# Seven block products in place of eight in units 1 to 7 of layer 2 of an FFT and two-layer MLP kernel

## Chip, cores and metric

One NeuronCore of a Trainium2 chip runs the kernel. The metric is the device time of one execution in microseconds (us); the number compared is the median over runs. Before the change it was 1027.38 us, the median of three runs from 1026.6 to 1029.3.

## What is computed

```python
X = np.fft.fft(np.fft.fft(x, axis=1), axis=2).real        # x: 2 x 3008 x 256
x = X.reshape(6016, 256)
h = x @ w_in                                              # layer 1, 256 x 2048
g = np.where(h >= 1, h, np.where(h <= -1, 0.0, (h + 1) ** 2 / 4))
x = g @ w_out                                             # 2048 x 256
h = x @ w_in2                                             # layer 2, 256 x 2048
g = np.maximum(0.01 * h, h)
return g @ w_out2                                         # 2048 x 256
```

## The kernel before

**Tiling.** Everything is held with features on the partitions and tokens along the free dimension. The 6016 tokens are 8 units of 752 (UT), each two halves of 376 columns (H4). The 2048 hidden features are 16 tiles of 128 (NF), called f. A step n is one f tile of one unit: layer 1 has steps 0 to 127 (N1 = 128), layer 2 steps 128 to 255. The Fourier transform comes first, in an order written out by hand, and its second stage is folded into layer 1's weights.

**Precision.** An fp32 operand is split into a rounded part ("high", type fp32r) and the difference ("low"). A product of two operands is three matmuls: high by high, high by low, low by high. So one 128 x 128 block of weights against one 128 x 376 block of tokens costs three matmuls.

**One step of layer 2** (`layer_2`, L672 on). `first_2` puts 12 matmuls (L556: two halves, two blocks of the 256 inputs, three each) into a pair of PSUM banks q. ScalarE writes 0.01 q to the SBUF tile s (L678), VectorE takes the maximum of q and s (L679). `high` (L574) rounds the step before on ScalarE, `low` (L578) forms its difference on GpSimd. `second` adds step n - 4 (LAG = 4) with 12 matmuls (L569) into four PSUM banks acc, which hold 256 outputs x 752 tokens of a unit; after the last f tile of a unit `store` copies them out, two on ScalarE (L597) and two on VectorE (L598). In layer 1 the copies stay in SBUF (tile y) and `split_y` (L606 on ScalarE, L607 on VectorE) makes the operands of layer 2; in layer 2 they go to the output by DMA.

**Layer 1's step** (`layer_1`) has 6 matmuls for its first product (L545), 12 for the second (L569), three VectorE operations on PSUM (L653, L656, L657), three activations on ScalarE and VectorE's maximum (L666).

**Order.** The kernel is under a manual schedule: every engine executes its instructions in the order in which they are written, and waits by semaphore where a tile isn't ready or a buffer isn't free. Side work hangs on a table `jobs`: `plan_at` puts a piece of work behind a given step. In layer 1 the second layer's first weights are loaded, converted from the 64-bit words in which they come (L210 to L223) and spilled to DRAM; from step 122 on `rf` reads them back, and L257 (ScalarE) and L261 (VectorE) split them into wc. The last weights (wd) are converted from step 125 to step 143 (L271 ScalarE, L275 VectorE).

**Buffers that the change touches.** Pool ps_ab has two pairs of PSUM banks, ps_acc four single banks; that is all eight. t3 holds three generations of gh and gl, t5 four tiles s, `by` eight units of the first layer's operands and later y, rw four tiles for loads.

Of the kernel before, what the change touches and what calls it, by code (L numbers as in the profile page):

```python
# [19 lines left out]
P = 128  # L20
# [138 lines left out]
def fnet_moe_kernel(ctx: ExitStack, tc: tile.TileContext, xpq, dft_e, dft_o, dft_d, pick,  # L159
# [23 lines left out]
    wb = {}  # L183
    bt = {}
# [49 lines left out]
    def first_weights(j):  # L234


        c = ToF32()
        t = {}

        def spill():  # L240
            c.rest()
            t["dram"] = sp.tile([P, 512], F32, name=f"w3f{j}")
            nc.sync.dma_start(out=t["dram"], in_=c.f32)

        def load():
            t["f32"] = rw.tile([P, 512], I64, tag="rw", name="rf").bitcast(F32)[:, :512]
            nc.sync.dma_start(out=t["f32"], in_=t["dram"])

        def views():
            v = t["w"].rearrange("p q (h e) f -> p q h e f", e=2)  # L250
            s = t["f32"].rearrange("p (q h f) -> p q h f", q=2, h=2)
            return [(v[:, q, :, 0, :], v[:, q, :, 1, :], s[:, q]) for q in range(2)]

        def high():
            t["w"] = new_wa(j, "wc")
            for hi, _, s in views():
                A.copy(hi, s)  # L257

        def low():
            for hi, lo, s in views():  # L260
                V.tensor_tensor(out=lo, in0=s, in1=hi.bitcast(F32), op=ALU.subtract)  # L261
            wa[j] = t["w"]

        return [lambda: c.load(w3, j), c.begin, c.exponent, c.sign, spill, load, high, low]
# [16 lines left out]
    with tc.manual_schedule():  # L281
# [249 lines left out]
        A.activation(warm[:, :1], warm[:, :1], CLAMP, scale=15.5)  # L531
# [5 lines left out]
        gh, gl, acc, yh, hp, rp, gp = {}, {}, {}, {}, {}, {}, {}  # L537
# [38 lines left out]
        def low(n):  # L576
            gl[n] = t3.tile([P, 2, H4], FR, tag="gl", name="gl")
            G.tensor_tensor(out=gl[n], in0=gp.pop(n), in1=gh[n].bitcast(F32), op=ALU.subtract)  # L578

        def store(n, first):  # L580

            u = n % N1 // NF
            if first:
                yt[u] = by.tile([P, 2, 2, H4], F32, tag="by", name=f"y{u}")
                dst = [yt[u][:, m] for m in range(2)]
            else:
                dst = [to.tile([P, 2, H4], F32, tag="o", name=f"o{u}{m}") for m in range(2)]
            if u == NU - 1 and not first:
                half = H4 // 2
                A.copy(dst[0][:, 0], acc[0][:, :H4])  # L590
                V.tensor_copy(dst[0][:, 1], acc[1][:, :H4])
                A.copy(dst[1][:, 0], acc[2][:, :H4])
                V.tensor_copy(dst[1][:, 1, :half], acc[3][:, :half])
                A.copy(dst[1][:, 1, half:], acc[3][:, half:H4])
# [178 lines left out]
```

## Time and profile before

| what | value |
| --- | --- |
| median of three runs | 1027.38 us (1026.6, 1027.38, 1029.3) |
| span of the profiled execution | 1029.2 us |
| TensorE (PE) busy | 1009.1 us, 98% of the span |
| weight loads (PEld) busy | 975.8 us, 95% |
| VectorE (DVE) | 610.2 us, 59% |
| ScalarE (ACT) | 623.7 us, 61% |
| GpSimd (POOL) | 491.8 us, 48% |

The profiled execution's own time isn't listed apart from its span; the highest of the three times, 1029.3, is 0.1 above that span. The shares are means over stages: the Fourier part fills about the first 110 us, layer 1 runs to about 500 us, layer 2 from there to the end. Matmuls overlap in the trace, so the mean duration of a matmul (334 ns) is longer than the time from one to the next; a stretch's time divided by its count gives that pace.

### The profile page before, as it was taken

Reading aid. Unit: us, or ns where it says so; the run is one execution under the profiler, and the core shown is the slowest. Engines: PE = TensorE matmul, PEld = TensorE weight load, DVE = VectorE, ACT = ScalarE, POOL = GpSimd, SP = SyncE. Lnnn points to the kernel's source line nnn. Section 1 sums busy time; section 2 is a strip of 40 time slices with the busy share of each in tenths; the row PEclk is TensorE's granted clock in tenths of the full one; section 3 lists DMA queues with packets and bytes.
Section 4 is the critical chain, followed back from the end, with each engine's and each line's share of the span. In section 5 each row is a group of like instructions: output and inputs, shape, how many; then the busy total and the mean of one; then the engine's idle time right before and its main releaser. Section 6 shows DMA issues by size and latency. Waiting matters only on the chain.

```text
span 1029.2 us, 14547 instructions
## 1 busy us (share of the span) xinstructions
PE 1009.1 (98%) x5660; PEld 975.8 (95%) x5660; DVE 610.2 (59%) x916; ACT 623.7 (61%) x975; POOL 491.8 (48%) x270
## 2 busy tenths in 40 slices
PE   7998999999999999999999999999999999999998
PEld 5657899999999999999999999999999999999998
DVE  5689999888888888888897232232323223232221
ACT  4357889888888888887775444444444444344443
POOL 1002876565655565655554444444444444444443
PEclk9799999999999999999999999999999999999999
DMA  9841000000100010101220000000000000000000
GB/s 298 295 129 62 1 1 21 12 32 2 42 11 11 32 32 2 52 1 62 82 93 1 32 1 31 1 1 31 1 7 24 1 31 2 1 31 1 31 1 31
DMA packets 12165, 39.25 MB, mean 38 GB/s; under 512 B 1472, under 2 KB 1472, under 8 KB 11840
## 3 DMA queue, kind: packets, MB, share of 16 engines
q1 hardware_dynamic: 11088, 34.79, 9.5%
q0 software_dynamic: 864, 3.15, 1.7%
q8 instruction: 44, 0.72, 0.3%
q10 hardware_dynamic: 144, 0.39, 0.1%
q14 instruction: 25, 0.20, 0.1%
HBM read 30.06 MB, written 8.26 MB: 37 GB/s over the span
## 4 chain that ended last, share of the span: by engine, by line
PE 88%; DVE 6%; ACT 3%; DMA 1%; issue 1%; ACTq 0%; DVEq 0%; SPq 0%
PE acc L569 47%; PE q L556 25%; PE p L545 11%; PE do L461 2%; DMA rw<-in_w_dram 1%; DVE r L666 1%; DVE tw L218 1%; DVE aa L653 1%; PE dc L426 1%; PE ds L427 1%; DVE h L656 1%; PE g L339 1%; DVE cw L223 1%; ACT gh L574 1%; DVE h L657 1%
## 5 line engine op out<-in xcount | busy, mean ns | idle before, releaser
L578 POOL TENSOR_TENSOR gl<-s,gh 128x752 fp32r<-128x752 f32 x128 | 235.0, 1836 | 288.8 <-ACT gh L574 288.8
L578 POOL TENSOR_TENSOR gl<-r,gh 128x752 fp32r<-128x752 f32 x128 | 243.7, 1904 | 188.6 <-ACT gh L574 129.0
L679 DVE TENSOR_TENSOR s<-q,s 128x752 f32<-128x752 f32 x128 | 120.2, 939 | 302.4 <-ACT s L678 302.2
L556 PE MATMUL q<-yh,wc 128*128 128x376 f32 x1536 | 284.7, 334 | 0.0
L569 PE MATMUL acc<-gh,wb 128*128 128x376 f32 x1024 | 281.1, 335 | 0.2
L569 PE MATMUL acc<-gh,wd 128*128 128x376 f32 x1024 | 278.9, 334 | 0.5 <-DVE y L598 0.5
L556 PEld LDWEIGHTS q<-yh,wc 128*128 128x128 f32 x1536 | 265.7, 188 | 0.0
L574 ACT CAST gh<-s 128x752 fp32r<-128x752 f32 x128 | 105.2, 822 | 146.3 <-PE acc L569 146.3
L569 PEld LDWEIGHTS acc<-gh,wb 128*128 128x128 f32 x1024 | 186.7, 188 | 3.3 <-ACT r L663 2.2
L569 PEld LDWEIGHTS acc<-gh,wd 128*128 128x128 f32 x1024 | 186.6, 188 | 0.8 <-DVE y L598 0.8
L678 ACT ACTIVATE s<-q 128x752 f32<-128x752 f32 x128 | 102.4, 800 | 138.6 <-PE q L556 138.6
L569 PE MATMUL acc<-gl,wb 128*128 128x376 f32 x512 | 172.1, 336 | 4.6 <-POOL gl L578 4.6
L569 PE MATMUL acc<-gl,wd 128*128 128x376 f32 x512 | 171.2, 334 | 0.0
L545 PE MATMUL p<-bt,wa 127*128 127x376 f32 (+3 forms) x768 | 154.5, 336 | 2.2 <-DVE bsc L484 1.4
L545 PEld LDWEIGHTS p<-bt,wa 128*128 128x128 f32 (+1 forms) x768 | 134.6, 189 | 3.7 <-ACT tw L210 1.7
L666 DVE TENSOR_TENSOR r<-h,r 128x752 f32<-128x752 f32 x128 | 127.7, 998 | 0.2 <-ACT r L670 0.2
L670 ACT ACTIVATE r<-r 128x752 f32<-128x752 f32 x128 | 106.8, 834 | 4.1
L569 PEld LDWEIGHTS acc<-gl,wb 128*128 128x128 f32 x512 | 96.3, 188 | 7.4 <-POOL gl L578 7.3
L574 ACT CAST gh<-r 128x752 fp32r<-128x752 f32 x128 | 103.2, 807 | 0.1
L659 ACT ACTIVATE r<-h 128x376 f32<-128x376 f32 x128 | 66.2, 517 | 60.2 <-DVE h L656 55.7
L653 DVE SCALAR_TENSOR_TENSOR aa<-ct,g,p 128x376 f32<-128x376 f32 (+1 forms) x128 | 77.3, 604 | 42.0 <-PE p L545 41.8
L569 PEld LDWEIGHTS acc<-gl,wd 128*128 128x128 f32 x512 | 96.0, 187 | 0.0
(79 smaller groups left out, 654.6 us busy)
## 6 DMA issues: line engine op xcount, KB each, us to landing
rw<-in_w_dram SPq DMA_DIRECT2D x32, 512.0 KB, 3.9
out_dram<-o SPq DMA_DIRECT2D x15, 376.0 KB, 2.8
x<-in_xpq_dram SPq DMA_DIRECT2D x6, 512.0 KB, 6.3
x<-in_xpq_dram POOLq DMA_DIRECT2D x6, 512.0 KB, 7.6
me<-in_dft_e_dram SPq DMA_DIRECT2D x4, 567.0 KB, 15.4
mo<-in_dft_o_dram SPq DMA_DIRECT2D x2, 1128.0 KB, 19.6
w3f<-cw SPq DMA_DIRECT2D x8, 256.0 KB, 2.2
rf<-w3f SPq DMA_DIRECT2D x8, 256.0 KB, 2.7
```

What stands on the lines that cost most here:

```text
L461: T.matmul(pe[:m, par, :H4], lhsT=weights(blk, lo, hi), rhs=mat[lo:hi, blk, c, :], start=(c == par and blk == 0), stop=(c == 2 and blk == 1))
L545: T.matmul(p[:, j, :n], lhsT=w[:m, 2 * j + x, :], rhs=b[:m, 2 * j + y, :n], start=(a == 0), stop=(a == 2))
L556: T.matmul(p[:, t, :H4], lhsT=w[:, 2 * d + x, :], rhs=y[d][:, z, t, :], start=(a == 0), stop=(a == 5))
L569: T.matmul(acc[k][:, :H4], lhsT=w[:, x, m * P:(m + 1) * P], rhs=y[:, t, :], start=(f == 0 and i == 0), stop=(f == NF - 1 and i == 2))
L574: A.copy(gh[n], gp[n])
L578: G.tensor_tensor(out=gl[n], in0=gp.pop(n), in1=gh[n].bitcast(F32), op=ALU.subtract)
L653: V.scalar_tensor_tensor(out=aa[:, :w], in0=ct[u][:, :w], scalar=g128[:, f:f + 1], in1=p[:, 0, :w], op0=ALU.mult, op1=ALU.add)
L659: A.activation(r[:, 0], h[:, 0], CLAMP, scale=15.5)
L666: V.tensor_tensor(out=g, in0=hp.pop(n - 1), in1=g, op=ALU.max)
L670: A.activation(r, r, AF.Square, scale=0.5 / 15.5, bias=0.5)
L678: A.activation(g, p, AF.Copy, scale=0.01)
L679: V.tensor_tensor(out=g, in0=p, in1=g, op=ALU.max)
```

## The change

Layer 2's first product treats two f tiles together. Its operands then are 2 x 2 blocks: the weights a11, a12, a21, a22 (f tile by input block) and the tokens b11, b12, b21, b22 (input block by half). Instead of eight block products it forms seven, with sums of weights s1 to s4 and sums of tokens t1 to t4:

- s1 = a21 + a22, s2 = s1 - a11, s3 = a11 - a21, s4 = a12 - s2
- t1 = b12 - b11, t2 = b22 - t1, t3 = b22 - b12, t4 = b21 - t2
- bank x collects a11 b11, then s2 t2, then s3 t3, then a22 t4; bank v collects s1 t1, then s4 b22; bank y holds a12 b21
- ScalarE copies x after its first product and v after its first product (tile av), and x after its second (tile bb); VectorE adds: h1 = (y + av, v + bb), second half of h2 = x + av; the last x is the first half of h2

This holds for units 1 to 7 (`layer_2_pair`, one call for two steps). Unit 0 keeps eight products (`layer_2`); its `low` runs on VectorE instead of GpSimd. The leaky maximum becomes one activation on ScalarE (`leaky`), VectorE's L679 is gone. Layer 1's result goes to DRAM and comes back as rows (`store`, `load_y`); GpSimd forms t1 to t4 (`mix_y`), ScalarE and VectorE split the seven operands of a unit (`split_high`, `split_low`). The weights' plain parts are kept by a DMA (`keep`), the rows are loaded a second time, VectorE forms s1 to s4 (`sum_1`, `sum_2`), and they are split (`mixed_high`, `mixed_low`). The accumulators are allocated once. `store` gives banks 0 and 1 to VectorE and banks 2 and 3 to ScalarE. From step 144 on the two PSUM pairs are four single banks, three of them used by a call of `layer_2_pair`. The clamp of layer 1 uses another saturating identity (limit 240 in place of 15.5, scales changed to match).

```diff
-            for hi, _, s in views():
-                A.copy(hi, s)
+        def high_of(key, nm):
+            t[key] = wp.tile([P, 4, 2, P], FR, tag="wa", name=f"{nm}{j}")
+            A.copy(t[key][:, :, 0, :], blocks(t["f32"])[:, t["at"]:t["at"] + 4])
+        def low_of(key):
...
+        def keep():
+            wt[j] = tri[j // 4].tile([P, 3, 2, P], FR, tag="wt", name=f"wt{j}")
+            nc.sync.dma_start(out=wt[j].bitcast(F32), in_=t["plain"][:, 0:3].bitcast(F32))
+        def sum_1():
+            V.tensor_tensor(out=s1, in0=a21, in1=a22, op=ALU.add)
+            V.tensor_tensor(out=s3, in0=a11, in1=a21, op=ALU.subtract)
+        def sum_2():
+            V.tensor_tensor(out=s2, in0=s1, in1=a11, op=ALU.subtract)
+            V.tensor_tensor(out=s4, in0=a12, in1=s2, op=ALU.subtract)
...
-        A.activation(warm[:, :1], warm[:, :1], CLAMP, scale=15.5)
+        A.activation(warm[:, :1], warm[:, :1], HOLD, scale=240.0)
...
+        def product(bank, w, y, start):
+            for a, (x, z) in enumerate(((0, 0), (0, 1), (1, 0))):
+                T.matmul(bank[:, :H4], lhsT=w[:, x, :], rhs=y[:, z, :], start=start and a == 0, stop=a == 2,
+                         skip_group_check=not start)
-        def second(n, f):
-            if f == 0:
+        def second(n, f, ks=range(4)):
+            if not acc:
...
-        def low(n):
+        def low(n, engine=G):
...
                 for t in range(2):
-                    A.copy(dst[0][:, t], acc[t][:, :H4])
-                    V.tensor_copy(dst[1][:, t], acc[2 + t][:, :H4])
+                    if part == 0:
+                        V.tensor_copy(o[:, t], acc[t][:, :H4])
+                    else:
+                        A.copy(o[:, t], acc[2 + t][:, :H4])
...
+        def mix_y(u, i):
+            b11, b12, b21, b22 = yr[u][:4]
...
+            out, x, y = ((t1, b12, b11), (t2, b22, t1), (t3_, b22, b12), (t4, b21, t2))[i]
+            G.tensor_tensor(out=out, in0=x, in1=y, op=ALU.subtract)
+        def split_high(u, i):
...
+            A.copy(ops[u][i // 2][:, i % 2, 0], yr[u][(0, 4, 5, 3, 6, 2, 7)[i]])
+        def split_low(u, i):
+            y = ops[u][i // 2][:, i % 2]
+            V.tensor_tensor(out=y[:, 1], in0=yr[u][(0, 4, 5, 3, 6, 2, 7)[i]], in1=y[:, 0].bitcast(F32),
+                            op=ALU.subtract)
...
-            plan_at(N1 - 6 + 2 * j, *zip((0, 3, 3), w3s[j][5:]))
-            plan_at(N1 - 3 + 2 * j, *zip((0, 1, 2, 2, 3, 4, 4), w4s[j]))
+            plan_all(N1 - 6 + 2 * j, (0, 3, 3, 4), plain)
+            plan_all(N1 + 8 + 2 * j, (0, 2, 3, 4, 5), mixed)
+            plan_at(N1 - 3 + 2 * j, *((x, k, s) for x, k, s in zip((0, 1, 2, 2, 3, 4, 4), "SSAVVAV", w4s[j])))
...
         for u in range(1, NU):
-            for d in range(2):
-                plan_at(N1 + NF * (u - 1) + 8 + 3 * d, (0, lambda u=u, d=d: split_y(u, d)))
+            plan_at(N1 + NF * (u - 1), (3, "S", lambda u=u: load_y(u)),
+                    *((5 + i, "G", lambda u=u, i=i: mix_y(u, i)) for i in range(4)),
+                    *((7 + i, "A", lambda u=u, i=i: split_high(u, i)) for i in range(7)),
+                    *((7 + i, "V", lambda u=u, i=i: split_low(u, i)) for i in range(7)))
...
-                A.activation(g, p, AF.Copy, scale=0.01)
-                V.tensor_tensor(out=g, in0=p, in1=g, op=ALU.max)
+        def leaky(out, h):
+            A.activation(out, h, AF.Prelu, alpha=0.01)
+        def layer_2(n):
...
+            leaky(g, p[:, :, :H4])
+            if n > N1:
+                high(n - 1)
+                low(n - 1, V)
+            sums(n)
+        def layer_2_pair(n):
+            new = n < 2 * N1
+            m1, m2 = n - 3, n - 2
...
+                product(x, a11, b11, True)
+                product(v, s1, t1, True)
+                A.copy(av[:, 0], x[:, :H4])
+                A.copy(av[:, 1], v[:, :H4])
+            todo(n, "S")
+            todo(n + 1, "S")
+            sums_of(m1, 0)
+            if last_x:
+                h, xp = last_x.pop()
+                leaky(h[:, 0], xp[:, :H4])
+                leaky(h[:, 1], h[:, 1])
+            if new:
+                product(x, s2, t2, False)
+                A.copy(bb, x[:, :H4])
+                product(v, s4, b22, False)
+                V.tensor_tensor(out=h1[:, 1], in0=v[:, :H4], in1=bb, op=ALU.add)
+            if n - 1 in gp:
+                high(n - 1)
+                low(n - 1)
+            sums_of(m1, 1)
+            todo(n, "AG")
+            if new:
+                product(x, s3, t3_, False)
+                V.tensor_tensor(out=h2[:, 1], in0=x[:, :H4], in1=av[:, 1], op=ALU.add)
+                product(y, a12, b21, True)
+                V.tensor_tensor(out=h1[:, 0], in0=y[:, :H4], in1=av[:, 0], op=ALU.add)
+            todo(n, "V")
+            sums_of(m2, 0)
+            if new:
+                leaky(h1, h1)
+                high(n)
+                low(n)
+            sums_of(m2, 1)
+            todo(n + 1, "AG")
+            if new:
+                product(x, a22, t4, False)
+                last_x.append((h2, x))
+            todo(n + 1, "V")
```

**Where the instructions stand now.** TensorE in a step of layer 2, before (wc the weights, yh the tokens of `first_2`; the same four rows and twelve of `second` make every step):

```order
L556 MATMUL q_4_8026<-yh_7660,wc_5191 128x376 x3
L556 MATMUL q_4_8026<-yh_7759,wc_5191 128x376 x3
L556 MATMUL q_4_8026<-yh_7660,wc_5191 128x376 x3
L556 MATMUL q_4_8026<-yh_7759,wc_5191 128x376 x3
L569 MATMUL acc_0_8046<-gh,wd_5184 128x376
L569 MATMUL acc_0_8046<-gl,wd_5184 128x376
L569 MATMUL acc_0_8046<-gh,wd_5184 128x376
```

and the start of a call of `layer_2_pair` (wt plain weights, ws summed ones, op the seven token operands):

```order
L581 MATMUL x_9276<-op_8531,wt_5602 128x376 x3
L581 MATMUL v_9278<-op_8531,ws_6208 128x376 x3
L592 MATMUL acc_798<-gh,wd_5549 128x376
L592 MATMUL acc_798<-gl,wd_5549 128x376
L592 MATMUL acc_798<-gh,wd_5549 128x376
L592 MATMUL acc_799<-gh,wd_5549 128x376
L592 MATMUL acc_799<-gl,wd_5549 128x376
L592 MATMUL acc_799<-gh,wd_5549 128x376
L581 MATMUL x_9276<-op_8606,ws_6208 128x376 x3
L581 MATMUL v_9278<-op_8606,ws_6208 128x376 x3
```

The seven products of three now stand in four places between the pieces of `second`, 21 and 24 matmuls in one call where two steps had 24 and 24; the whole program has 5377 matmuls instead of 5545.

ScalarE in three steps of layer 2, before:

```order
L678 ACTIVATE s<-q_4_8026 128x752
L574 CAST gh<-s 128x752
L678 ACTIVATE s<-q_5_8062 128x752
L574 CAST gh<-s 128x752
L678 ACTIVATE s<-q_6_8094 128x752
L574 CAST gh<-s 128x752
```

and in one call of `layer_2_pair` (two steps), without side work:

```order
L807 COPY av<-x_7059 128x376
L808 COPY av<-v_7061 128x376
L753 ACTIVATE s<-x_6990 128x376
L753 ACTIVATE s<-s 128x376
L818 COPY bb<-x_7059 128x376
L597 CAST gh<-s 128x752
L753 ACTIVATE s<-s 128x752
L597 CAST gh<-s 128x752
```

Two steps had four instructions of 752 columns here; one call has three of 752 and five of 376. Three of the copies read a bank that TensorE goes on adding to.

VectorE in the first unit of layer 2, two steps before:

```order
L679 TENSOR_TENSOR s<-q_8_5456,s 128x752
L218 SCALAR_TENSOR_TENSOR tw<-rw,tw 128x512
L223 SCALAR_TENSOR_TENSOR cw<-rw,tw 128x512
L607 TENSOR_TENSOR yh_5493<-y_1905,yh_5493 128x752
L679 TENSOR_TENSOR s<-q_9_5496,s 128x752
L275 TENSOR_TENSOR wd_5528<-cw,wd_5528 128x2x256
L214 TENSOR_SCALAR tw<-tw 128x512
L261 TENSOR_TENSOR wc_5535<-rf,wc_5535 128x2x128 x2
```

and two steps now:

```order
L601 TENSOR_TENSOR gl<-s,gh 128x752
L277 TENSOR_TENSOR rf<-rf 128x128
L278 TENSOR_TENSOR rf<-rf 128x128
L220 SCALAR_TENSOR_TENSOR tw<-rw,tw 128x512
L225 SCALAR_TENSOR_TENSOR cw<-rw,tw 128x512
L665 TENSOR_TENSOR op_5561<-ry,op_5561 128x376
L601 TENSOR_TENSOR gl<-s,gh 128x752
L282 TENSOR_TENSOR rf<-rf 128x128
L283 TENSOR_TENSOR rf<-rf 128x128
L305 TENSOR_TENSOR wd_5639<-cw,wd_5639 128x2x256
L216 TENSOR_SCALAR tw<-tw 128x512
L260 TENSOR_TENSOR wc_5646<-rf,wc_5646 128x4x128
```

The maximum is replaced by the difference gl; the sums of weights and the splits of the tokens of unit 1 have come in between. ScalarE's order has one ACT_TABLE_LOAD, at its start, before and now.

## Rows read from the trace of the kernel before

**Rows 1.** Page, parts 1 and 2: busy time, and TensorE's granted clock in 40 slices.

```profile
PE 1009.1 (98%) x5660; PEld 975.8 (95%) x5660; DVE 610.2 (59%) x916; ACT 623.7 (61%) x975; POOL 491.8 (48%) x270
PEclk9799999999999999999999999999999999999999
```

**Rows 2.** Busy time by stage: stretch, its length, engines (instructions), clock, DMA share, GB/s.

```profile
0.00:110.00 110.00, 97.39 (x391) 69.80 (x392) 85.13 (x180) 58.46 (x116) 18.06 (x16) 0.94 0.57 183
300.00:400.00 100.00, 99.93 (x578) 99.06 (x577) 85.64 (x142) 84.19 (x139) 60.27 (x32) 1.00 0.06 20
506.60:1024.90 518.30, 518.12 (x3012) 517.81 (x3012) 182.08 (x191) 230.67 (x307) 229.53 (x126) 1.00 0.05 18
600.00:700.00 100.00, 100.00 (x584) 100.00 (x583) 29.30 (x29) 42.55 (x54) 43.72 (x25) 1.00 0.02 9
```

**Rows 3.** Page, part 4: the chain that ended last, by engine.

```profile
PE 88%; DVE 6%; ACT 3%; DMA 1%; issue 1%; ACTq 0%; DVEq 0%; SPq 0%
```

**Rows 4.** TensorE groups by line: busy, mean ns, idle before and what ended it.

```profile
L556 PE MATMUL q<-yh,wc 128*128 128x376 f32 x1536 | 284.7, 334 | 0.0
```

**Rows 5.** Timeline inside layer 2: start, length (us), instruction, idle before.

```profile
645.07 2.23 PE L556 MATMUL q<-yh,wc 128*128 128x376 f32 x12
645.26 0.82 ACT L574 CAST gh<-s 128x752 fp32r<-128x752 f32 x1 [1.20 <-PE acc L569]
646.23 1.82 POOL L578 TENSOR_TENSOR gl<-s,gh 128x752 fp32r<-128x752 f32 x1 [2.31 <-ACT gh L574]
647.39 0.80 ACT L678 ACTIVATE s<-q 128x752 f32<-128x752 f32 x1 [1.30 <-PE q L556]
```

**Rows 6.** ScalarE groups by line, shapes apart.

```profile
L597 ACT COPY o<-acc 128x376 f32<-128x376 f32 x14 | 5.9, 473 | 0.0
L659 ACT ACTIVATE r<-h 128x376 f32<-128x376 f32 x128 | 66.2, 517 | 60.2 <-DVE h L656 55.7 <-POOL gl L578 3.0 <-issue 0.2
L670 ACT ACTIVATE r<-r 128x752 f32<-128x752 f32 x128 | 106.8, 834 | 4.1
L574 ACT CAST gh<-s 128x752 fp32r<-128x752 f32 x128 | 105.2, 822 | 146.3 <-PE acc L569 146.3
```

**Rows 7.** VectorE and GpSimd groups by line, shapes apart.

```profile
L656 DVE TENSOR_TENSOR h<-aa,p 128x376 f32<-128x376 f32 x128 | 69.9, 546 | 4.4
L505 DVE TENSOR_TENSOR bt<-bs,bt 128x376 fp32r<-128x376 f32 x4 | 2.0, 548 | 0.2
L666 DVE TENSOR_TENSOR r<-h,r 128x752 f32<-128x752 f32 x128 | 127.7, 998 | 0.2 <-ACT r L670 0.2
L382 DVE TENSOR_TENSOR xt<-pc 126x129 f32<-126x129 f32 x12 | 3.4, 286 | 0.0
L578 POOL TENSOR_TENSOR gl<-s,gh 128x752 fp32r<-128x752 f32 x128 | 235.0, 1836 | 288.8 <-ACT gh L574 288.8
```

**Rows 8.** Timeline of GpSimd and VectorE at the start of layer 2.

```profile
505.20 1.86 POOL L578 TENSOR_TENSOR gl<-s,gh 128x752 fp32r<-128x752 f32 x1 [1.10 <-ACT gh L574]
505.29 0.93 DVE L679 TENSOR_TENSOR s<-q,s 128x752 f32<-128x752 f32 x1
507.05 0.68 DVE L275 TENSOR_TENSOR wd<-cw,wd 128x512 fp32r<-128x512 f32 x1
507.65 0.42 DVE L214 TENSOR_SCALAR tw<-tw 128x512 int32<-128x512 int32 x1
514.18 1.84 POOL L578 TENSOR_TENSOR gl<-s,gh 128x752 fp32r<-128x752 f32 x1 [2.07 <-ACT gh L574]
514.59 1.97 DVE L275 TENSOR_TENSOR wd<-cw,wd 128x512 fp32r<-128x512 f32 x1 [1.08 <-ACT wd L271]
```

**Rows 9.** Timeline of TensorE and VectorE where layer 2's first sums begin.

```profile
506.14 0.99 DVE L598 COPY y<-acc 128x376 f32<-128x376 f32 x2
506.73 0.44 PE L569 MATMUL acc<-gh,wd 128*128 128x376 f32 x1 [0.48 <-DVE y L598]
```

**Rows 10.** Page, part 6: loads of weight words, KB each, median us to landing.

```profile
rw<-in_w_dram SPq DMA_DIRECT2D x32, 512.0 KB, 3.9
```

More of the change, by code (lines that the diff above doesn't have):

```diff
@@ L183, in fnet_moe_kernel @@
     wb = {}
+    wt = {}
+    tri = []
     bt = {}
@@ L245, in load @@
         def load():
[L246 to L252, printed above, removed]
+            t["f32"] = rw.tile([P, 512], I64, tag="rw", name="rf").bitcast(F32)
+            nc.sync.dma_start(out=t["f32"][:, :512], in_=t["dram"])
@@ L259, in low @@
         def low():
[L260 to L264, printed above, removed]
+            low_of("plain")
+        def keep():
+            wt[j] = tri[j // 4].tile([P, 3, 2, P], FR, tag="wt", name=f"wt{j}")
+            nc.sync.dma_start(out=wt[j].bitcast(F32), in_=t["plain"][:, 0:3].bitcast(F32))
+        def sum_1():
+            a11, a12, a22, a21, s1, s2, s3, s4 = (blocks(t["f32"])[:, i] for i in range(8))
+            V.tensor_tensor(out=s1, in0=a21, in1=a22, op=ALU.add)
+            V.tensor_tensor(out=s3, in0=a11, in1=a21, op=ALU.subtract)
@@ new lines, in sum_2, with mixed_high, mixed_low @@
+        def sum_2():
+            a11, a12, a22, a21, s1, s2, s3, s4 = (blocks(t["f32"])[:, i] for i in range(8))
+            V.tensor_tensor(out=s2, in0=s1, in1=a11, op=ALU.subtract)
+            V.tensor_tensor(out=s4, in0=a12, in1=s2, op=ALU.subtract)
+        def mixed_high():
+            t["at"] = 4
+            high_of("mixed", "ws")
+        def mixed_low():
+            low_of("mixed")
+        return ([("S", lambda: c.load(w3, j)), ("A", c.begin), ("V", c.exponent), ("V", c.sign), ("V", spill)],
+                [("S", load), ("A", high), ("V", low), ("S", keep)],
+                [("S", load), ("V", sum_1), ("V", sum_2), ("A", mixed_high), ("V", mixed_low)])
@@ L574, in high, with store @@
             A.copy(gh[n], gp[n])
-        def low(n):
+        def low(n, engine=G):
             gl[n] = t3.tile([P, 2, H4], FR, tag="gl", name="gl")
-            G.tensor_tensor(out=gl[n], in0=gp.pop(n), in1=gh[n].bitcast(F32), op=ALU.subtract)
-        def store(n, first):
+            engine.tensor_tensor(out=gl[n], in0=gp.pop(n), in1=gh[n].bitcast(F32), op=ALU.subtract)
+        def store(n, part):
             u = n % N1 // NF
[L583 to L588, printed above, removed]
-                half = H4 // 2
[L590 to L594, printed above, removed]
+            first = n < N1
+            last = u == NU - 1 and not first
+            if part == 0:
+                ot[u] = [to.tile([P, 2, H4], F32, tag="o", name=f"o{n // NF}{m}") for m in range(2)]
+            o = ot[u][part]
+            if last and part == 0:
+                A.copy(o[:, 0], acc[0][:, :H4])
+                V.tensor_copy(o[:, 1], acc[1][:, :H4])
+            elif last:
+                half = H4 // 2
+                A.copy(o[:, 0], acc[2][:, :H4])
+                V.tensor_copy(o[:, 1, :half], acc[3][:, :half])
+                A.copy(o[:, 1, half:], acc[3][:, half:H4])
@@ new lines, in store, with load_y @@
+            if first:
+                yt[u, part] = sp.tile([P, UT], F32, name=f"y{u}{part}")
+            queue = nc.scalar if last and part else nc.sync
+            queue.dma_start(out=yt[u, part] if first else out[part, :, u * UT:(u + 1) * UT],
+                            in_=o.rearrange("p t n -> p (t n)"))
+        def load_y(u):
+            yr[u] = []
+            for d in range(2):
+                if u == 1:
+                    y = th.tile([P, 2, H4], F32, tag="h", name="ry").rearrange("p t n -> p (t n)")
+                else:
+                    y = rw.tile([P, 512], I64, tag="rw", name="ry").bitcast(F32)[:, :UT]
+                nc.sync.dma_start(out=y, in_=yt[u, d])
+                yr[u] += [y] if u == 0 else [y[:, :H4], y[:, H4:]]
```

168 lines of the change are left out of this document (102 added, 66 removed).

## Prediction

> **What bounds the kernel now.** I read the page first. TensorE is busy for 98% of the span, the other engines for 48 to 61% [rows 1]; the reader is to see that one engine is full and that its clock stands at the top digit (2.4 GHz) in all slices but the second. Busy time alone does not say what paces it, so the table by stage comes next [rows 2]: in the first 110 us TensorE has 97.39 busy us and the clock is 0.94; in layer 1, 99.93 of 100 with VectorE and ScalarE at some 85; in layer 2, 100.00 of 100, VectorE at 29 and ScalarE at 43. Layer 2 is where the change lies, and there nothing but TensorE can be the bound. The chain that ended last says the same, PE 88% [rows 3], and the first product's group has no idle time in front of it over 1536 matmuls [rows 4].
>
> So the price of a matmul is read from this stretch: 3012 of them from 506.60 to 1024.90 us in 518.12 us, **172.0 ns each**. (The groups' mean of 334 ns is no price: matmuls overlap.) Weight loads are busy as long as matmuls; each matmul has its own, so both counts fall together. A step of 24 is 4.13 us, two steps 8.26.
>
> **What is removed.** Per call of the new function, three matmuls of 48. There are 7 units x 8 calls = 56 calls, so 168 matmuls, as the programs' counts of 5545 and 5377 say too. 168 x 172.0 ns = **28.9 us**. A call has 45 matmuls, 7.74 us. All else is worth what it makes TensorE wait.
>
> **ScalarE in a call.** Copies av, av and bb from PSUM, 376 columns: 3 x 0.473 (the eviction at L597). The leaky function on two halves: nothing in the trace ran it. Its nearest rows are other functions of the same size: 0.473 for a copy from PSUM, 0.517 for the clamp, 0.834 for the square on 752 [rows 6]. I take these, since clamp, square and copy hardly differ; below them I see no reason for a gain, above them the trace gives no end, and that end is a rival. So 0.47 + 0.52 + 0.83, and two casts of 0.822. Sum 4.88 us. No table load comes with it, since the order has one, as before. Side work per call: seven split casts of a unit, priced as the clamp, 7 x 0.517 / 8 = 0.45, and two output copies, 2 x 0.473 / 8 = 0.12. In all 5.45 of 7.74 us: covered.
>
> **The new waits, by position in a call.** From one engine's end to the next one's start the trace shows 0.09 us (TensorE to ScalarE, 647.30 to 647.39) and 0.15 us (ScalarE to GpSimd, 646.08 to 646.23) [rows 5]; I take 0.15. Position k is k x 0.172 us after the call's start.
> - Bank x is done at position 3 (0.52), copied from 0.67 to 1.14; TensorE adds s2 t2 to it at position 12 (2.06). Bank v: done 1.03, copied to 1.65, needed at position 15 (2.58). The second copy of x: done at 2.58, copied 2.73 to 3.20, needed at position 24 (4.13). Margins 0.92, 0.93, 0.93 us. What could fill ScalarE at that time: the cast of the call before ends at 7.81, a split cast at 8.33, which is 0.59 into this call; and the two leaky halves from 1.65 to 2.65. They fit, just.
> - The add from x after s3 t3 (position 27, 4.64) ends by 5.34 with 0.546 for a VectorE operation on PSUM [rows 7]; TensorE needs the bank at 42 (7.22).
> - The chain behind h1: bank y at position 30 (5.16), add to 5.86, leaky to 6.84, cast to 7.81, GpSimd's difference of 1.836 to 9.8; its first reader stands 30 matmuls into the next call, at 12.9. Margin 3.1. Behind h2: casts end at about 4.0 of the next call, the difference at 6.0, read at 8.9. Margin 2.9.
>
> VectorE has 3 x 0.546 + 7 x 0.548 / 8 and two evictions per unit, some 2.3 us a call; GpSimd 2 x 1.836 and four small differences per unit, each between 0.92 (half of 752 columns) and 1.84: 4.1 to 4.6 us. Neither is near 7.74. Queues: a split parked on VectorE stands in front of the next call's first add, which is ready at about 3.2 and not missed before 5.2. On SP the row loads and the stores stand in program order; a row is asked for two steps or more before its use, 8 us, against the 3.9 that a larger load took to land [rows 10], so a store that waits for its eviction delays nothing that is due.
>
> **First unit.** VectorE now forms the differences (0.998 at most, two SBUF operands) beside the conversions. The fullest step: difference 1.00, last weights 0.68, shift 0.42, plain split 0.68, two sums 2 x 0.286, token split 0.55 [rows 7, 8]: 3.9 us of 4.13. A difference is read two steps after it is made, so even a slip of some us has 4 to 8 us of cover; without that cover each us over 4.13 would be paid once per step. Cost 0, bounds 0 and 3. GpSimd is idle there except for four differences.
>
> **Seams.** Before, the layers' seam had one wait of 0.48 us for an eviction [rows 9]. Now the copies of banks 0 and 1 follow the difference on VectorE: 0.15 + 0.82 + 0.15 + 1.0 + 0.54 = 2.66 us after the last sum against 12 matmuls = 2.06, a wait of about 0.6. Change 0.1: nothing. At later seams 18 matmuls lie between: no wait, as before. Layer 1's evictions only change engine order, and its DMAs have no reader nearby. Cost 0, bounds -0.5 and +1.
>
> **Sum.** -28.9 against the profiled span of 1029.2 gives 1000.3; that span is 1.8 above the median of the runs, so against 1027.4 the forecast is **998.5 us**. Its own range is 996 to 1002: the three runs spread from 0.8 below to 1.9 above their median, and the bounds of seams and first unit are -0.5 and +4.
>
> **VectorE and GpSimd beside each other.** At 514.59 VectorE's difference of two SBUF tiles took 1.97 us while GpSimd worked from 514.18 to 516.02; alone it took 0.68. The maximum at 505.29, one operand in PSUM, took 0.93 with GpSimd at work beside it [rows 8]. So the three adds of a call, each with one PSUM operand, keep their price, and splits and weight sums may be held up by one GpSimd operation, 1.84. The Trainium skill, GPSIMD Engine Reference, section 8 (Key points), says that GpSimd shares its SBUF interfaces with VectorE and contends with instructions of two SBUF inputs. The trace agrees (1.97 against 0.68); going by that rule for every such instruction, the first six calls would be the ones to suffer, which is the first rival.
>
> **Rivals.**
> 1. *VectorE is held up until TensorE waits.* In the first six calls of unit 1 VectorE has 3 x 0.546, four sums of 0.286, two splits (0.68 and 0.55): 4.0 us. If it is held up twice for 1.84 each call, 7.7 of 7.74: full, and its adds come late. Price up to 1 us a call, 6 us; the same margins of 0.9 us eaten at unit ends, where two evictions join, would add 1 us at 7 seams: at most 13 in all, 1002 to 1012; I say **1006**. For it: 1.97 in the rows. Against: GpSimd is free for 3 us of a call, and the adds have 2 us of cover.
> 2. *Slower than before: the leaky function is dear on ScalarE.* Its three instructions take 1.82 of ScalarE's 5.45 us a call, and two of them stand in front of the second copy of x, for which TensorE stops at position 24. The gain is gone, with 3.1 us on top, at 32 / 56 = 0.57 us a call: ScalarE would need 8.31 a call, 2.86 more, which is the leaky function at 2.6 times these rows. At three times it needs 5.45 + 3.64 = 9.09, 1.35 over TensorE's 7.74 in each of 56 calls, 76 us: **1074**. Against: no function of ScalarE in the trace costs more than a copy by over 0.05 us at 376 columns.
> 3. *It doesn't shorten the stage.* If a matmul into a bank that is read between its products starts later by what three matmuls save, 0.52 us a call, time stays at **1027**. Against: the order keeps 9 to 18 matmuls between them.
>
> **How the numbers follow.** Forecast, 996 to 1002: 0.77. Rival 1, up to 1012: 0.14. Rival 2: 0.04. Rival 3: 0.01. Below 996, from waits before layer 2 that I did not count: 0.04. A measurement of this kernel tells about 0.3% (3.1 us) from no change. Faster 0.95 (the forecast, rival 1 and below), same 0.01, slower 0.04. From 996 to 1007 most of rival 1 is taken in, and less than 2 in 10 left out.
>
> **What would show it.** Right: layer 2's units 1 to 7 with TensorE at 100% and 61.9 us a unit instead of 66.0; matmuls 168 fewer; leaky halves at 0.47 and 0.52 us; ScalarE at 70%. Wrong: idle time of TensorE in front of the products, ended by ScalarE's copies (rival 2 or margins too small) or by VectorE's adds (rival 1); VectorE late in the first unit, ended by gl; a clock below 1.00 in layer 2.

## The result and the profile after

The changed kernel takes **998.57 us** (median of four runs: 995.45, 995.48, 1001.66, 1002.38) against 1026.99 for the kernel before (four runs, 1026.3 to 1029.3): a ratio of **0.9713**, 95% interval 0.9672 to 0.9753 (the two medians alone divide to 0.9723). The forecast was 998.5. The size came from the predicted place; that it agrees to 0.1 us is luck, as the four runs show: they lie in two pairs, 995.5 and 1002, and the median lies between them, so that three of the four times are outside the forecast's own range of 996 to 1002 though their median is inside. The pairs differ in the mean granted clock, 0.997 and 0.998 against 0.989 and 0.991. Each of these four times is 1.8 us above its span.

The page of the changed kernel: busy time, granted clock in 40 slices, the chain by engine.

```profile
PE 979.7 (98%) x5492; PEld 945.9 (95%) x5492; DVE 626.1 (63%) x1038; ACT 712.5 (71%) x1234; POOL 494.2 (49%) x283
...
PEclk9699999999999999999999999999999999999999
...
PE 88%; DVE 7%; ACT 2%; DMA 2%; issue 1%; ACTq 0%; DVEq 0%; SPq 0%
```

168 matmuls fewer than in [rows 1], and the chain is TensorE's as in [rows 3]. By stage, columns as in [rows 2]:

```profile
0.00:110.00 110.00, 98.10 (x387) 69.99 (x387) 83.94 (x179) 57.41 (x113) 17.55 (x16) 0.92 0.56 179
300.00:400.00 100.00, 99.93 (x578) 99.06 (x577) 85.70 (x143) 84.18 (x138) 60.28 (x33) 1.00 0.12 40
507.60:995.30 487.70, 487.55 (x2844) 487.25 (x2844) 200.27 (x316) 319.76 (x569) 237.22 (x141) 1.00 0.12 40
600.00:700.00 100.00, 100.00 (x586) 100.00 (x585) 36.46 (x55) 66.07 (x120) 51.75 (x30) 1.00 0.09 32
```

Layer 2 is still TensorE's alone: 100.00 of 100, with ScalarE up from 43 to 66. The stage took 518.30 us [rows 2], now 487.70: 30.6 less, where 28.9 were counted. The start of each layer's sums (count, min/median/max ns, first and last start), before:

```profile
L569 PE MATMUL acc<-gh,wb x1024: 327/333/442, 94.1 to 503.9; 128*128 128x376 f32 x171
...
L569 PE MATMUL acc<-gh,wd x1024: 327/333/439, 506.7 to 1024.5; 128*128 128x376 f32 x171
```

and after:

```profile
L592 PE MATMUL acc<-gh,wb x1024: 328/333/444, 95.3 to 504.9; 128*128 128x376 f32 x171
...
L592 PE MATMUL acc<-gh,wd x1024: 327/333/443, 507.7 to 994.9; 128*128 128x376 f32 x171
```

So the two profiled spans (1029.2 and 999.9) differ by +1.2 us ahead of layer 1's sums, -0.2 from there to layer 2's, -30.6 in layer 2 and +0.3 in the tail. The +1.2 is put down to the head's clock: the change ran at 1.2 GHz for 17.0 us there, the kernel before for 13.7 (below), and with the clock kept up by filler matmuls the two heads end 0.1 us apart (89.0 and 88.9 us).

The groups that the sum priced (line, tile, count, busy us, mean ns, idle before), after:

```profile
L592 PE MATMUL acc<-gh,wd 128*128 128x376 f32 x1024 | 287.7, 333 | 0.4 <-DVE o L622 0.4
...
L753 ACT ACTIVATE s<-s 128x752 f32<-128x752 f32 x56 | 46.7, 833 | 94.2 <-DVE s L830 94.2
...
L753 ACT ACTIVATE s<-s 128x376 f32<-128x376 f32 x56 | 29.1, 519 | 0.0
L753 ACT ACTIVATE s<-x 128x376 f32<-128x376 f32 x56 | 27.5, 491 | 0.2 <-PE x L581 0.2
...
L818 ACT COPY bb<-x 128x376 f32<-128x376 f32 x56 | 26.5, 473 | 16.4 <-PE x L581 16.4
...
L820 DVE TENSOR_TENSOR s<-v,bb 128x376 f32<-128x376 f32 x56 | 30.8, 550 | 152.2 <-PE v L581 152.1
...
L665 DVE TENSOR_TENSOR op<-ty,op 128x376 fp32r<-128x376 f32 x28 | 39.4, 1406 | 27.4 <-ACT op L661 27.4
...
L656 POOL TENSOR_TENSOR ty<-ry 128x376 f32<-128x376 f32 x14 | 16.2, 1159 | 16.7 <-DMA ry<-y 16.7
```

The leaky function costs 0.49, 0.52 and 0.83 us, within 0.02 of what [rows 6] gave for a copy, a clamp and a square. The additions cost 0.55, as in [rows 7]. What is dearer is VectorE's difference of two SBUF tiles (L665), 1.41 us. One call of the pairs in the timeline, after:

```profile
842.89 1.88 DVE L665 TENSOR_TENSOR op<-ty,op 128x376 fp32r<-128x376 f32 x1 [1.75 <-ACT op L661]
843.21 0.47 ACT L807 COPY av<-x 128x376 f32<-128x376 f32 x1 [0.35 <-PE x L581]
...
844.09 0.49 ACT L753 ACTIVATE s<-x 128x376 f32<-128x376 f32 x1
844.47 0.52 ACT L753 ACTIVATE s<-s 128x376 f32<-128x376 f32 x1
...
844.55 0.68 PE L581 MATMUL x<-op,ws 128*128 128x376 f32 x3
...
845.26 0.47 ACT L818 COPY bb<-x 128x376 f32<-128x376 f32 x1 [0.28 <-PE x L581]
...
846.61 0.68 PE L581 MATMUL x<-op,ws 128*128 128x376 f32 x3
...
848.43 0.83 ACT L753 ACTIVATE s<-s 128x752 f32<-128x752 f32 x1 [1.57 <-DVE s L830]
...
850.91 0.47 ACT L807 COPY av<-x 128x376 f32<-128x376 f32 x1 [0.34 <-PE x L581]
```

x is copied by 843.68 and added to at 844.55, copied again by 845.73 and added to at 846.61: margins 0.87 and 0.88 us, where 0.92 and 0.93 were worked out. The next call's copy starts 7.70 us after this one's.

### The profile page after: what moved, and what is told of

Its sections match the earlier page's. It is cut to its first block, busy times and chain, and to the rows that moved or that the text cites. A ratio compares the mean times of both kernels' runs of the same rounds, so it can differ in the third digit from the quotient of the medians.

```text
span 999.9 us, 14700 instructions
## 1 busy us (share of the span) xinstructions
PE 979.7 (98%) x5492; PEld 945.9 (95%) x5492; DVE 626.1 (63%) x1038; ACT 712.5 (71%) x1234; POOL 494.2 (49%) x283
## 4 chain that ended last, share of the span: by engine, by line
PE 88%; DVE 7%; ACT 2%; DMA 2%; issue 1%; ACTq 0%; DVEq 0%; SPq 0%
PE acc L592 50%; PE x L581 12%; PE p L575 11%; PE v L581 6%; PE q L766 3%; PE y L581 3%; DMA rw<-in_w_dram 2%; PE do L491 1%; DVE r L737 1%; DVE aa L724 1%; DVE tw L220 1%; DVE h L727 1%; PE dc L456 1%; DVE h L728 1%; PE ds L457 1%
## 5 line engine op out<-in xcount | busy, mean ns | idle before, releaser
L601 POOL TENSOR_TENSOR gl<-s,gh 128x752 fp32r<-128x752 f32 x113 | 205.9, 1822 | 240.0 <-ACT gh L597 239.3
L592 PE MATMUL acc<-gh,wd 128*128 128x376 f32 x1024 | 287.7, 333 | 0.4 <-DVE o L622 0.4
L753 ACT ACTIVATE s<-s 128x752 f32<-128x752 f32 x112 | 75.7, 676 | 94.2 <-DVE s L830 94.2
L820 DVE TENSOR_TENSOR s<-v,bb 128x376 f32<-128x376 f32 x56 | 30.8, 550 | 152.2 <-PE v L581 152.1
L581 PE MATMUL x<-op,ws 128*128 128x376 f32 x336 | 75.8, 334 | 0.0
L581 PE MATMUL v<-op,ws 128*128 128x376 f32 x336 | 75.7, 333 | 0.0
```

Source lines behind the costliest of these rows:

```text
L581: T.matmul(bank[:, :H4], lhsT=w[:, x, :], rhs=y[:, z, :], start=start and a == 0, stop=a == 2, skip_group_check=not start)
L592: T.matmul(acc[k][:, :H4], lhsT=w[:, x, m * P:(m + 1) * P], rhs=y[:, t, :], start=(f == 0 and i == 0), stop=(f == NF - 1 and i == 2))
L601: engine.tensor_tensor(out=gl[n], in0=gp.pop(n), in1=gh[n].bitcast(F32), op=ALU.subtract)
L753: A.activation(out, h, AF.Prelu, alpha=0.01)
L820: V.tensor_tensor(out=h1[:, 1], in0=v[:, :H4], in1=bb, op=ALU.add)
```

## The experiments

From the fourth experiment on, all kernels carry the filler matmuls that it adds, so that most of their runs compare at one clock.

**Eight products in the new order.**

```diff
                 product(y, a12, b21, True)
+                product(y, a12, b21, True)
```

> The new order with eight block products: y's product stands twice in each of the 56 calls, 168 matmuls more, all else as in the change. Theory A (the gain is the count of matmuls times TensorE's pace, and nothing else of the change matters): 168 x 171.3 to 172.0 ns = 28.8 to 28.9 us more than the change, so 1027.5 us, the time before. Theory B (a part of the gain comes from elsewhere, the new order or the freed VectorE): the time stays below that of the kernel before by as much; the profiles suggest some 1.7 us, since a matmul in units 1 to 7 started every 171.28 ns after the change and every 171.95 ns before it. Theory C (the pairs' order hides a loss that the saved matmuls cover): the time lies above 1030 us.

Measured: 1025.62 us (10 runs), ratio to before 0.9994 (0.997 to 1.0018). The gain is the count: A, against C. Runs at one clock show a part of B as well: the six at 0.997 or more have a median of 1024.8, 29.4 above the change's pair at that clock, and nine of the kernel before in the same clock range 1026.0. The matmuls still start every 171.40 ns.

**The leaky function two and three times.** (`k` is 2 or 3; slope 1 leaves the value as it is.)

```diff
-                leaky(h[:, 0], xp[:, :H4])
+                for _ in range(k):
+                    leaky(h[:, 0], xp[:, :H4])
+                for _ in range(k - 1):
+                    A.activation(h[:, 1], h[:, 1], AF.Prelu, alpha=1.0)
                 leaky(h[:, 1], h[:, 1])
...
+                for _ in range(k - 1):
+                    A.activation(h1, h1, AF.Prelu, alpha=1.0)
                 leaky(h1, h1)
```

> Each of the three leaky instructions of a call of the pairs runs twice (the same function, the result unchanged), ScalarE's price of the leaky function doubled. Theory A (the prediction's sum: what counts is ScalarE's busy time of 5.45 us a call, 7.27 with the doubled instructions, against 7.70): no change, 998.6 us, the point of decision being 2.6 times. Theory B (a loop decides, not a sum: the copy of x must end before TensorE adds s3 t3, that product and y's must end before ScalarE's leaky function on h1, then its cast, the next call's copies and leaky halves stand in front of the next copy of x; its slack in the profile of the change is 0.75 + 0.35 + 0.28 = 1.4 us a call, at 843 to 854 us, and the doubling takes 1.7 to 2.0 us): TensorE waits 0.3 to 0.6 us in each of some 56 calls, 1015 to 1033 us, most likely 1025.

> As the doubled leaky function, but each of its three instructions three times. Theory A (busy sum, the prediction's second rival: 9.09 us of ScalarE against 7.74 a call): 1.35 us x 56 = 76 us, 1074 us. Theory B (the loop with 1.4 us of slack, to which the two further copies add 3.4 to 4.0 us): 2.0 to 2.6 us a call, 113 to 147 us, most likely 1125 us.

Measured: twice, 1007.40 us (4 runs), ratio 0.9806 (0.9769 to 0.9843); its run at a clock of 0.999 took 1003.23, 7.8 more than the change at 0.998, 0.14 us a call on average. Three times: 1105.06 (one run, 0.998), 109.6 more, 1.96 us a call. Waits in units 1 to 7 (total, times, longest), twice, of the weight loads:

```profile
PEld x L581 <- ACT bb L821: 6.9, 24, 0.3
```

and three times, of the matmuls, the weight loads and ScalarE:

```profile
PE x L581 <- ACT bb L821: 73.2, 55, 1.4
PE x L581 <- ACT av L807: 7.5, 24, 0.6
PEld x L581 <- ACT bb L821: 90.3, 55, 1.7
PEld x L581 <- ACT av L807: 21.2, 54, 0.9
ACT s L838 <- DVE s L833: 54.2, 54, 1.3
```

Both times fall between the theories. Doubled, the time is nearer to A's "no change" than to B's 1025; tripled, it is nearer to B's 1125 than to A's 1074. The place is B's in both: TensorE and its weight loads stop for ScalarE's second copy of x, doubled in 24 of the 56 calls. Even tripled, ScalarE isn't full, as a sum would have it: it waits 1.0 us in each call for VectorE's addition h1, and is busy for 350.08 of the 400 us from 560 to 960. The third copy of the function costs 1.82 us a call, the second only 0.14. The three instructions take 1.84 us, so the loop had some 1.7 us of slack (an estimate; two more copies less 1.96 give the same), a little over the 1.4 read from the timeline.

**Fillers in the head.** `fill k` puts k matmuls on zeros into a bank that is overwritten later.

```diff
-2, fill 3, w1_exponent 3, w1_begin 0, w1_join 3, g_high 2, w1_exponent 0, load_w1 5, g_product 3, load_me 1,
+2, fill 8, w1_exponent 3, w1_begin 0, w1_join 3, g_high 2, w1_exponent 0, load_w1 5, g_product 3, fill 6, load_me 1,
```

> The change with 11 more filler matmuls on zeros in TensorE's two gaps of the first 25 us (17.3 to 19.8 and 21.8 to 24.4 us of its profile, where it waits for VectorE's conversions); nothing else. Theory A (the 6 to 7 us between the runs of the change, 995.5 and 1002, come from the stretch of half clock that follows these gaps, 25.5 to 42.5 us in the profiled run, with TensorE busy in all of it from 28 us on): the stretch is shorter or gone, the granted clock at 0.997 or more, and all runs lie at 992 to 996 us. Theory B (the low clock has another cause, or the fillers only push the work behind them): the runs still lie in two groups at 995.5 and 1002, or all are later by up to 1 us.

Measured: 995.27 us (994.86 to 995.52, 4 runs), ratio 0.9695 (0.9674 to 0.9716), clock 0.999 to 1.000: A for these four; later kernels with the same fillers still had runs at a lower clock (below). The head of the change without fillers, by stretch:

```profile
15.20:25.50 10.30, 5.33 (x24) 4.12 (x23) 5.52 (x10) 3.69 (x9) 0.00 (x0) 1.00 1.04 298
25.50:42.50 17.00, 16.33 (x37) 9.92 (x36) 12.66 (x37) 3.99 (x8) 0.86 (x1) 0.50 1.00 384
```

and with the fillers:

```profile
15.20:25.50 10.30, 10.30 (x49) 8.81 (x47) 6.06 (x12) 3.76 (x9) 0.00 (x0) 1.00 1.04 297
25.50:42.50 17.00, 15.20 (x70) 9.77 (x68) 15.25 (x41) 6.38 (x14) 0.86 (x1) 1.00 1.01 386
```

TensorE was busy for 5.33 of 10.30 us; it waited twice, 5.0 us in all, for VectorE's conversions. Then the clock stood at 1.2 GHz for 17 us, in which it did 37 matmuls instead of 70. In the profile with the gaps filled it stays at 2.4 GHz.

**The kernel before with the same fillers.** The edit is the one above.

> The kernel before with the same 11 filler matmuls in the gaps of the first 25 us as the run with the fillers on the change (995.27 us, granted clock 0.999 to 1.000 in every run), so that both can be compared at one clock. All runs should lie within 1 us of each other at a granted clock of 0.999 or more. Theory A (the change is worth 168 matmuls at 172.0 ns, no more): 995.3 + 28.9 = 1024.2 us. Theory B (it is worth 30.4 us, which is the difference between the two kernels' runs at a clock of 0.998, 1025.9 and 995.45; the 1.5 us beyond the count come from a pace of 171.3 instead of 172.0 ns over the 2688 matmuls of units 1 to 7 less the 168): 1025.7 us.

Measured: 1025.73 us (10 runs, one of them at 0.995 and 1029.48), ratio 0.9980 (0.9959 to 1.0002). Against 995.27 the change is worth 30.5 us at one clock: B. The two were measured on different chips, on which the kernel before without these fillers agrees to 0.1 us (medians of 1025.9 and 1026.0 at a clock of 0.996 or more).

**The leaky function alone**, on the kernel before with fillers (clamp to HOLD as in the change):

```diff
-                A.activation(g, p, AF.Copy, scale=0.01)
-                V.tensor_tensor(out=g, in0=p, in1=g, op=ALU.max)
+                A.activation(g, p, AF.Prelu, alpha=0.01)
```

> One part of the change alone, on the kernel before with the fillers: in layer 2 the leaky maximum is one ScalarE instruction on both halves instead of a scaled copy on ScalarE and a maximum on VectorE, and layer 1's clamp takes the wider form that the change uses; eight products everywhere, the order as before. Theory A (TensorE bounds layer 2, and neither engine's work there is on the path): within 0.5 us of the kernel before with the fillers, 1024.2 to 1025.7. Theory B (the faster pace of a matmul after the change, 171.28 against 171.95 ns, comes from VectorE no longer reading two PSUM banks in each step): 1.7 us less than that, and the pace 171.3. A table load of ScalarE inside the steps would show as 1 us or more in each and cost nothing in time.

Measured: 1026.80 us (10 runs), ratio to before 0.9983 (0.9960 to 1.0006). Half of the runs had a clock of 0.994 or 0.995; the other five have a median of 1024.6, 1.0 below the kernel before with fillers. The seam's wait of 0.5 us is gone, which is half of that 1.0; where the other half comes from isn't shown. The pace is 171.94: against B, and A in its range of times, though the 1.0 is more than the 0.5 us that A allowed.

**Six products.** `product(y, ...)` is left out and h1's first half is taken from v, so this half of the result is not computed.

```diff
-                product(y, a12, b21, True)
-                V.tensor_tensor(out=h1[:, 0], in0=y[:, :H4], in1=av[:, 0], op=ALU.add)
+                V.tensor_tensor(out=h1[:, 0], in0=v[:, :H4], in1=av[:, 0], op=ALU.add)
```

> The change with the fillers, but y's product left out (six products, 42 matmuls a call; h1's first half is taken from v's bank, so this part of the result is not computed). Theory A (TensorE is still the only bound, and the loop through ScalarE, some 6.0 us of a call of 7.70, has 1.2 us left at 7.19): 168 x 171.3 = 28.8 us less than the change with the fillers, 966.5 us. Theory B (the seven-product order is already close to its next bound: ScalarE's copies or VectorE's additions stop TensorE): less gain, 975 to 985 us, with idle time of TensorE in front of the products of x.

Measured: 967.90 us (4 runs), ratio 0.9410 (0.9365 to 0.9455); 966.62 at a clock of 1.0, 28.7 below seven products. A: TensorE is the only bound at six products too.

**The pairs' difference on VectorE.**

```diff
                 high(n - 1)
-                low(n - 1)
+                low(n - 1, V)
...
                 high(n)
-                low(n)
+                low(n, V)
```

> The change with the fillers, but in the pairs the difference gl is formed by VectorE instead of GpSimd (two of 752 columns a call; 1.0 instead of 1.82 us each). GpSimd then has only the four small differences of a unit, and VectorE's operations with two SBUF operands are hardly held up (1.4 to 1.9 us beside GpSimd in the profile of the change, 0.55 alone). Theory A (nothing of VectorE or GpSimd is on the path): 995.3 us, within 0.5. Theory B (hold-ups cost the change something, the prediction's first rival at a small scale): faster by up to 2 us. Theory C (VectorE, with the difference parked in front of its additions, delays the loop): slower by 5 us or more.

Measured: 995.75 us (4 runs), ratio 0.9684 (0.9643 to 0.9725): A. VectorE's difference L665 from 560 to 990 us, in the change and, held up no more, here:

```profile
L665 DVE TENSOR_TENSOR op<-ty,op 128x376 fp32r<-128x376 f32 x24 | 37.2, 1550 | 27.4 <-ACT op L661 27.4
```

```profile
L665 DVE TENSOR_TENSOR op<-ty,op 128x376 fp32r<-128x376 f32 x24 | 13.0, 542 | 0.0
```

0.54 us instead of 1.55, and no time comes of it.

**The first unit's difference on GpSimd again.**

```diff
                 high(n - 1)
-                low(n - 1, V)
+                low(n - 1)
```

> One part of the change undone, on the change with the fillers: in the first unit of layer 2 the difference gl is again formed by GpSimd (1.82 us) instead of VectorE (1.0 us). Theory A (the prediction's cost 0 for this part: the difference is read two steps after it is made, so neither engine is on the path): 995.3 us, within 0.5; at the layers' seam TensorE's one wait of 0.4 us may go, since VectorE no longer makes a difference ahead of the copies out of the accumulators. Theory B (GpSimd, with the differences and the next unit's small ones, holds up VectorE's conversions, which are full at 3.9 of 4.13 us a step): TensorE waits in the first unit, up to 1.3 us in some of its steps, 997 to 1008 us.

Measured: 997.09 us (995.12, 995.14, 999.03, 1000.01), ratio 0.9716 (0.9681 to 0.9752); the first two at a clock of 0.999 or more: A, and TensorE has no wait at the seam. The first unit from 510 to 550 us by engine, and its conversion L225 by line, with GpSimd's differences beside it:

```profile
510.00:550.00 40.00, 40.00 (x235) 40.00 (x234) 36.47 (x45) 28.77 (x46) 25.06 (x15) 1.00 0.41 125
```

```profile
L225 DVE SCALAR_TENSOR_TENSOR cw<-rw,tw 128x512 int32<-128x512 int32 x5 | 10.1, 2029 | 0.2
```

and with the differences on VectorE (the next run):

```profile
510.00:550.00 40.00, 40.00 (x235) 40.00 (x234) 31.44 (x51) 28.68 (x47) 4.60 (x4) 1.00 0.43 143
```

```profile
L225 DVE SCALAR_TENSOR_TENSOR cw<-rw,tw 128x512 int32<-128x512 int32 x5 | 3.5, 692 | 0.2
```

VectorE, the third engine of the row, is less busy (31.44 of 40) when it makes the differences itself than when GpSimd makes them (36.47).

**Three more fillers**, and the same kernel once more.

```diff
-g_low 2, w1_join 0, g_high 3, fold_x 0 0, g_product 0, w1_begin 6, g_high 0, g_low 0, load_x 1 0, col_copy 0
+g_low 2, w1_join 0, g_high 3, fold_x 0 0, g_product 0, fill 3, w1_begin 6, g_high 0, g_low 0, load_x 1 0, col_copy 0
```

> The change with the 11 fillers and three more in the gap that was left, 25.8 to 27.2 us. Of 24 runs of four kernels with 11 fillers that were near enough to compare (the change, the kernel before, GpSimd's difference moved, leaky alone) some still had a granted clock of 0.993 to 0.995 and lay 4 to 5 us later; in the one of them that was profiled the half clock ran from 29.1 to 39.3 us, behind that gap. Theory A (that gap is what is left of the cause): every run at 0.999 or more, 994.5 to 996 us. Theory B (the clock falls for reasons that TensorE's gaps don't set): some runs at 0.993 to 0.997 and 999 to 1001 us, as with the 11 fillers.

> The change with 14 fillers once more, for more runs: five runs without one at a lower clock are few, where about three in ten of those with 11 fillers had one. Theory A (TensorE's gaps in the first 28 us are what lets the clock fall): again every run at 0.999 or more and 994.5 to 996 us. Theory B (chance): one run or two in five at 0.993 to 0.997 and 998 to 1001 us.

Measured: **995.18 us** (994.91 to 995.61), ratio 0.9689 (0.9666 to 0.9712), and 995.51 (995.22 to 995.97), ratio 0.9680 (0.9657 to 0.9703); all ten runs at 0.999 or more. Of the 46 runs of the seven kernels with 11 fillers 12 were at 0.995 or lower; without them it was 9 of 19 runs (the change, eight products, the leaky function two and three times) and 21 of 56 of the kernel before in the same series. So 14 fillers against none is clear; what the last three add to the 11 is likely but not shown, since at 12 in 46 ten runs in a row without one come about once in twenty times.

**The pairs' order of banks with eight products**, on the kernel before with fillers: `first_2` works on one input block at a time, and the sums come in two parts.

```diff
-                p = first_2(u, f)[:, :, :H4]
+                q = psum_pair(f"q{u}_{f}")
+                first_2(u, f, q, 0)
+                second(m, m % NF, (0, 1))
+                first_2(u, f, q, 1)
+                p = q[:, :, :H4]
...
-            sums(n)
+            second(m, m % NF, (2, 3) if n < 2 * N1 else range(4))
```

> The kernel before with the fillers, eight products, but layer 2's matmuls in the order of the pairs: three into one bank, then the next bank, and the sums' 12 in two parts of 6 between them, instead of 6, 6 and 12. It asks where the 0.66 ns a matmul (171.94 against 171.28) come from that are left after the count; neither VectorE's maximum nor GpSimd's differences made them. Theory A (the order of banks): a pace of 171.3 in layer 2, 2900 matmuls x 0.66 ns = 1.9 us less than the kernel before with the fillers, 1023.5 us. Theory B (the operands of the products, or how weights follow each other in SBUF): pace 171.9, 1025.5 us.

Measured: 1027.91 us (10 runs), ratio 1.0012 (0.9994 to 1.0030), 2.2 above the kernel before with fillers. The time missed both forecasts, the pace is A's: 171.21 ns between starts, gaps over 250 ns left out. What it wins there it loses at the units' ends, where the next unit's first sums now stand 6 matmuls behind the last and wait for the copies out of the accumulators:

```profile
PE acc L564 <- ACT o L592: 1.8, 7, 0.3
```

The starts show some 0.52 us lost at each of the seven unit ends (a pause of 0.59 and one of 0.28 in place of 0.17 each), 3.6 us in all against some 2.1 won by the pace (2900 x 0.73 ns).

## Why the prediction was right, point by point

- **168 matmuls x 172.0 ns = 28.9 us, nothing else on the path.** Right: eight products in the new order bring the time back, six take off another 28.7. Mis-sized by 1.7 us: the pace was taken as fixed. In the same 400 us of units 1 to 7 the trace of before has

```profile
560.00:960.00 400.00, 400.00 (x2328) 400.00 (x2327) 119.83 (x121) 170.52 (x218) 175.98 (x98) 1.00 0.03 12
```

 and that of after

```profile
560.00:960.00 400.00, 400.00 (x2338) 400.00 (x2337) 153.91 (x238) 263.82 (x477) 215.53 (x128) 1.00 0.08 27
```

 ten matmuls more. By their starts that is 171.95 and 171.28 ns; 2520 x 0.67 = 1.7 us. With 28.9 it is the 30.6 of the stage. Neither VectorE's load (leaky alone: 171.94) nor GpSimd's (difference moved: 171.28) sets it; the order of the matmuls does (171.21 with eight products and the same operands). Whether that is the banks that follow each other, the weights that do, the groups of three or the divided sums wasn't tried, nor why it is so.
- **The step from span to time.** "That span is 1.8 above the median" set an execution against runs at another clock. A run's time is 1.8 us above its own span, so the profiled execution of before took about 1031 (an estimate; its own time isn't on record). That this offset equals the one used is chance. At one clock the change is worth 30.5 us, not the 28.9 forecast and not the 28.4 between the medians. The forecast's range had no term for the pace, and for the clock only the spread of three runs, 0.8 below to 1.9 above, where the change's two pairs lie 6.5 us apart; the median of 998.57 is where the two errors meet.
- **ScalarE, 5.45 of 7.74 us.** Prices right, to 0.03 us. Busy is 66% instead of 70%: neighbouring instructions overlap, 0.49 us long but 0.38 apart (844.09, 844.47). From 560 to 960 us their durations add up to 286.4 us, 5.5 a call, and the busy time is 263.82.
- **Margins 0.92 and 0.93 us.** Measured 0.87 and 0.88; TensorE has no wait in units 1 to 7.
- **First unit, cost 0.** Right in time. The fullest step was to take VectorE 3.9 us; from 515.98 to 520.10 it was busy for all 4.12, held up beside GpSimd's small differences (the split of the last weights took 1.50 us here, 0.68 alone), and TensorE did not wait. Undone, this part is worth nothing either.

```profile
515.49 1.43 POOL L656 TENSOR_TENSOR ty<-ry 128x376 f32<-128x376 f32 x1 [16.67 <-DMA ry<-y]
...
515.97 1.50 DVE L305 TENSOR_TENSOR wd<-cw,wd 128x512 fp32r<-128x512 f32 x1
```

- **Layers' seam.** A wait of about 0.6 was worked out, 0.4 measured, 0.48 before [rows 9].
- **Rival 1, VectorE held up.** The hold-up is there, within the 1.84 us that was allowed for each (1.88 us for 0.54 at 842.89; in the first unit with GpSimd's differences 2.03 for 0.69), but nothing waits for it: taking it away is worth 0. The Trainium skill's rule that GpSimd contends with VectorE's instructions of two SBUF inputs (GPSIMD Engine Reference, section 8, Key points) is borne out: L665 takes 1.55 us beside GpSimd and 0.54 without, while the additions with one operand in PSUM stay at 0.55.
- **Rival 2, leaky dear.** It did not come, and the point where it would decide was wrong. It added up ScalarE's busy time and let it fill TensorE's 7.74 us. But ScalarE, TensorE and VectorE wait for each other in a ring: copy of x, third product of x, y, the additions, leaky, cast, the next call's copies. The waits of the tripled run are its links: TensorE for bb, ScalarE for the addition. With slack of 1.7 us a call and a gain of 0.54, the gain is gone at some 2.2 times the function's price (an estimate: 2.24 us more on 1.84), not 2.6; at three times the loss is 110 us over the change, not 76.
- **Rival 3.** Out: from 560 to 960 us no matmul starts more than 0.19 us after the one before it, so there is no gap in front of a product into a bank that is read between.

## What to carry to other kernels

Where one engine is at 100% of a stage and its waits are zero, a count times the pace between starts prices removed work (here 28.9 of 30.6 us); read the pace from the stretch that is changed, and expect it to move a little when the order does. A rival's price needs the ring of waits that it lies in, not the sum of an engine's busy time. When runs differ by more than a few tenths of a per cent, put their granted clocks beside them before comparing medians.

## What the runs showed of the hardware

- TensorE's clock fell to 1.2 GHz in the head after a stretch in which TensorE was busy about half of the time (5.33 of 10.30 us after, 7.88 of 13.70 before), and stayed there while TensorE was busy almost throughout: 13.7 us in the profile of before (28.3 to 42.0 us), 17.0 after, 10.2 with the leaky function alone. Runs at a lower mean clock take 3 to 7 us more than others of the same kernel, and whether it falls differs from run to run. With 14 more matmuls on zeros in the gaps ten runs of ten stayed at 0.999 or more; with 11, 12 of 46 were at 0.995 or lower.
- An operation of VectorE with two SBUF operands can take three times as long beside GpSimd (2.03 for 0.69 us), so that moving work to GpSimd made VectorE busier: 36.47 of 40 us instead of 31.44.
- The leaky function with a slope runs on ScalarE at the price of a copy, 0.49 us for 376 columns from PSUM, and keeps the table that was loaded.
- The pace of dense matmuls with a weight load each depends on their order, 171.2 against 171.9 ns at 376 columns with eight products.
